# Forgetting attention with a SwiGLU block: tanh's table set loaded later, batch 0's first copies in two parts, first stage in a new order

## The chip, the cores and the metric

The kernel runs on one core of one Trainium2 chip. Its time is device microseconds (us), the median of several runs. The engines are TensorE (PE for matmuls and transposes, PEld for its weight loads), VectorE (DVE), ScalarE (ACT), GpSimd (POOL) and SyncE (SP). All five run at once, each through its own instructions in the order in which they were issued; they wait for one another by semaphores. SP, ACT and POOL also issue the DMAs here.

## The reference

Eight batches with eight heads each, 576 positions, 64 numbers per head; then 4608 tokens of 512 numbers through a SwiGLU block with 1536 hidden columns. Inputs and output are float32.

```
scores = q @ k^T / 8
cum    = cumsum(log(clip(f, 1e-4, 1)))              # one forget gate per position
scores = scores + cum[i] - cum[j], causal, then softmax, then @ v
x      = the heads side by side, [4608, 512]
out    = (silu(x @ w_gate) * (x @ w_val)) @ w_out
```

## The kernel before, in words

**The planner.** The kernel first collects its work as operations and then issues them. `Plan` (L35 to L196) is a list scheduler that runs on the host while the program is built. Each operation has engines on which it may run with a cost for each, operations that it comes after, buffers that it takes and frees, and a key. `plan.run` (L1276) goes through a modelled time: whenever an engine is free by the model, it issues on that engine the ready operation with the lowest key. So costs, keys and ready times set the order of the instructions on every engine and, where an operation has two engines, which of them does it. On the chip each engine then keeps that order and waits where the model was wrong. `ORDER` (L1352) holds a key for each of some 600 operations by its number; where it names an operation, it replaces the key written beside that operation. The memset of `idle` is operation 3: it isn't named in this table and keeps its own key of -1e9 (L526).

**Idle matmuls.** `_fill` (L68) puts matmuls of a constant tile `idle` into gaps that the model sees on PE (`dummy`, L1272), from 0.55 to 22 us of modelled time. They compute nothing that is used. The model doubles PE's costs for the first 6 us (TWARM).

**Logs and gates.** f is loaded in four parts and clipped (L359), ACT takes the logs (L363), DVE sums them up by a scan (L367), splits the sums into bfloat16 parts (`hi` L372 and the following), and ACT or DVE make from them the rows by which a score matmul adds the decays (`choose`, L392 on ACT, L394 on DVE: the picks). This is done in two parts, of 256 and of 320 positions.

**Batch 0.** Its q and k come by POOL's DMAs, two heads groups g of two pairs of heads each. `turn_two` (L558, matmuls at L563) transposes them on PE, for each pair and each of q and k as 18 times two 64 x 64 blocks into one PSUM bank; `straighten_two` (L566) copies the 576 columns of the bank into QK, on ACT (L328) or DVE (L330), whichever the planner finds free. `score2` (L710, matmuls at L722 and L730) makes the scores of two heads at once, in four banks of columns called i = 0 to 3; `soft` (L826) is exp on ACT (`expo`, L738) and the causal mask on POOL (L747); `weigh` (L751, matmul L761) multiplies by v. The scores of i = 0 only need the first 256 positions, yet they wait for all of `q_ready`.

**Batch 1** is transposed on PE as well, with 128 rows at a time (`turn` L574, matmul L579; `straighten` L582). From batch 2 on, transposing DMAs do this (`queries`, L680). v is held in VB, whose padding `blank` fills (L467, L471).

**Feed forward.** `unit` (L1057) is a gate matmul group (L919), tanh on ACT (L930; silu is made of tanh), a value group (L919 too), and two products on DVE (L940, L943). `finish` multiplies by w_out (L985). The first token tile's first four columns groups are done in two halves, 256 wide, later ones are 512 wide. Attention of later batches is mixed in between, so that PE always has either. At the operation ALONE the kernel changes from tanh to Silu (`whole`, L932), with a table load of its own (`turn_table`, L935).

**Table loads.** ACT holds one set of function tables. `o_ln` (L523) is a Ln of one number ahead of all logs, which makes the compiler load the set with Ln; `o_warm` (L531) is an Exp of one number behind the logs, which loads the set with exp and tanh. The exps of i = 0 of batch 0 wait for `o_warm` (in `soft`, L828).

## Time and profile before

| | us |
|---|---|
| median of 3 runs | 376.16 (375.9 to 376.44) |
| profiled execution | 376.5 |
| its span in the trace | 374.5 |
| instructions in the span | 9689 |
| PE busy | 368.0 (98%) |
| DVE busy | 256.9 (69%) |
| ACT busy | 212.5 (57%) |
| POOL busy | 169.5 (45%) |

Times inside the trace count from the span's start. In a timeline row the first two numbers are the start of a run of alike instructions and the time until the last of them ended; then come the engine, the line, the operation, what it writes and reads, the shape and the count, and, in brackets, idle time ahead of it with what ended it. In a row of a view by stages each engine has its busy time and its count of instructions, then the granted clock, a DMA share and GB/s. Matmuls overlap: a group's time divided by its count, less what one takes alone, gives the step from one to the next.

### The profile page before, as it was taken

The page shows a single profiled execution, that of the slowest core. Times are in us where ns is not written, and L with a number is a line of the kernel's source. Part 1 is how long each engine was busy: PE and PEld are TensorE (multiplying, and loading weights), DVE is VectorE, ACT ScalarE, POOL GpSimd, SP SyncE. Part 2 cuts the span into 40 slices and gives each one's busy share as a digit, 9 for nine tenths or more (in the row PEclk, how much of TensorE's full clock was granted, in tenths as well). Part 3 has the DMA queues.
Part 4 walks back from the last instruction along what each step waited for, and adds up shares of the span by engine and source line. Part 5 has one row for each costly group of instructions (what it writes and reads, how often), then busy time and mean ns, then how long its engine had stood idle before and what let it go on. Part 6 is the DMA issues. An engine that isn't in the chain of part 4 may idle for free.

```text
span 374.5 us, 9689 instructions
## 1 busy us (share of the span) xinstructions
PE 368.0 (98%) x3715; PEld 249.2 (67%) x3715; DVE 256.9 (69%) x605; ACT 212.5 (57%) x436; POOL 169.5 (45%) x396
## 2 busy tenths in 40 slices
PE   7899999999999999999999999999999999999996
PEld 5667666455789646875578955587666964584586
DVE  7878987499937699548973769845888246617633
ACT  6999953256755647756566556676874233333321
POOL 8897554135565416684249533566440400040021
PEclk9999999999999999999999999999999999999999
DMA  8999998896959997999979999898530120011012
GB/s 144 190 200 194 206 217 143 169 215 121 174 106 234 212 161 111 170 221 181 200 152 200 126 234 196 155 150 212 105 38 19 58 84 2 1 58 56 0 57 86
DMA packets 125179, 52.04 MB, mean 139 GB/s; under 512 B 111838, under 2 KB 119582, under 8 KB 124366
## 3 DMA queue, kind: packets, MB, share of 16 engines
q1 hardware_dynamic: 108638, 36.15, 50.8%
q0 software_dynamic: 16288, 15.14, 27.1%
q8 instruction: 29, 0.48, 0.6%
q14 instruction: 16, 0.13, 0.1%
q10 hardware_dynamic: 208, 0.14, 0.1%
HBM read 38.56 MB, written 17.07 MB: 149 GB/s over the span
## 4 chain that ended last, share of the span: by engine, by line
PE 93%; ACT 3%; DVE 2%; issue 1%; POOL 0%; DVEq 0%; ACTq 0%
PE ps L919 43%; PE ps L985 17%; PE ps L704 10%; PE ps L761 8%; PE ps L926 6%; PE ps L998 3%; PE ps L992 3%; PE ps L722 1%; PE ps L579 1%; PE ps L778 1%; ACT PT L738 1%; ACT QK L328 1%; PE ps L730 0%; ACT xT L363 0%; ACT PTa L738 0%
## 5 line engine op out<-in xcount | busy, mean ns | idle before, releaser
L738 ACT ACTIVATE PT<-ps 128x384 bf16<-128x384 f32 (+2 forms) x192 | 90.8, 510 | 15.6 <-PE ps L704 10.7
L919 PE MATMUL ps<-xT,wv 128*128 128x512 bf16 (+1 forms) x400 | 99.3, 370 | 0.0
L919 PE MATMUL ps<-xT,wg 128*128 128x512 bf16 (+1 forms) x400 | 99.1, 370 | 0.0
L943 DVE SCALAR_TENSOR_TENSOR hh<-th,ps 128x512 bf16<-128x512 f32 (+1 forms) x100 | 65.9, 662 | 19.4 <-PE ps L919 15.9
L930 ACT ACTIVATE th<-ps 128x512 f32<-128x512 f32 (+1 forms) x82 | 47.2, 577 | 51.5 <-PE ps L919 44.8
L747 POOL TENSOR_SCALAR_AFFINE_SELECT PT<-PT 128x128 bf16<-128x128 bf16 (+1 forms) x192 | 54.6, 291 | 41.6 <-ACT PT L738 35.9
L940 DVE SCALAR_TENSOR_TENSOR th<-th,ps 128x512 f32<-128x512 f32 (+1 forms) x82 | 53.7, 655 | 14.7 <-ACT th L930 14.4
L704 PE MATMUL ps<-QK 68*128 68x256 bf16 x392 | 62.8, 261 | 0.1
L919 PEld LDWEIGHTS <-wg 128*128 128x128 bf16 x400 | 37.7, 97 | 34.2
L919 PEld LDWEIGHTS <-wv 128*128 128x128 bf16 x400 | 37.4, 97 | 34.5
L747 POOL TENSOR_SCALAR_AFFINE_SELECT PTa<-PTa 128x256 bf16<-128x256 bf16 x64 | 26.9, 423 | 63.9 <-ACT PTa L738 62.9
L976 DVE TENSOR_TENSOR su<-hh 128x512 bf16<-128x512 bf16 (+1 forms) x126 | 46.6, 404 | 1.0
L985 PEld LDWEIGHTS <-su 128*128 128x128 bf16 x420 | 40.4, 98 | 5.3
L761 PE MATMUL ps<-VB,PT 128*128 128x65 bf16 x768 | 41.4, 193 | 0.1
L704 PEld LDWEIGHTS <-QK 68*128 68x128 bf16 x392 | 31.8, 97 | 13.9 <-issue 0.3
L1018 POOL TENSOR_TENSOR ot<-ot 128x256 f32<-128x256 f32 x14 | 10.1, 724 | 63.8 <-ACT ot L1011 63.8
L761 PEld LDWEIGHTS <-PT 128*128 128x128 bf16 x768 | 34.1, 97 | 7.0 <-POOL PT L747 1.0
L738 ACT ACTIVATE PTa<-ps 128x384 bf16<-128x384 f32 x64 | 30.9, 488 | 12.6 <-PE ps L704 11.7
L933 ACT ACTIVATE th<-ps 128x512 f32<-128x512 f32 x30 | 17.9, 596 | 33.1 <-PE ps L919 27.7
L773 DVE TENSOR_TENSOR xn<-ps,rc 128x320 bf16<-128x320 f32 (+2 forms) x72 | 32.4, 453 | 2.1
L985 PE MATMUL ps<-wt,su 128*128 128x256 bf16 x252 | 32.9, 272 | 0.0
L1011 ACT ACTIVATE ot<-ps 128x512 f32<-128x512 f32 x28 | 16.7, 597 | 27.9 <-PE ps L985 26.5
(101 smaller groups left out, 407.0 us busy)
## 6 DMA issues: line engine op xcount, KB each, us to landing
out_dram<-ot SPq DMA_DIRECT2D x35, 256.0 KB
natv<-in_v_dram SPq DMA_DIRECT2D x25, 256.0 KB
qk_d<-in_q_dram POOLq DMA_DIRECT2D x24, 144.0 KB, 4.3
qk_d<-in_k_dram POOLq DMA_DIRECT2D x24, 144.0 KB, 4.8
wv<-in_moe_w_val_dram POOLq DMA_DIRECT2D x3, 512.0 KB, 10.7
wg<-in_moe_w_gate_dram POOLq DMA_DIRECT2D x3, 512.0 KB, 12.1
wo<-in_moe_w_out_dram POOLq DMA_DIRECT2D x4, 384.0 KB, 13.7
VB<-in_v_dram POOLq DMA_DIRECT2D x7, 128.0 KB, 9.1
```

What stands on the lines that cost most here:

```text
L704: nc.tensor.matmul(s[:, c : c + w], QK[:KR, hqk[p].i, 1, j * S + kt * P : j * S + (kt + 1) * P], QK[:KR, hqk[p].i, 0, j * S + q0 : j * S + ...
L738: nc.scalar.activation(place(h, i)[:, OFFS[i] : OFFS[i] + c], ps(bs)[:, :c], AF.Exp, scale=0.125)
L747: nc.gpsimd.affine_select(out=d, in_=d, pattern=pat, compare_op=ALU.is_ge, fill=0.0, base=0, channel_multiplier=-1,)
L761: nc.tensor.matmul(o[:, lo : lo + D + 1], pt[:, c : c + P], VB[hvb[b].i][:, kt, hb, : D + 1], start=first and n == 0, stop=last and n == l ...
L773: nc.vector.tensor_mul(XN[bx.i][:, qb : qb + nq, j], o, r)
L919: nc.tensor.matmul(ps(bf)[:, a:b], w[:, ko, fc * P : (fc + 1) * P], xT[:, ko, at : at + b - a], start=ko == 0 and a == 0, stop=ko == KD - ...
L926: nc.tensor.matmul(ps(bf)[:, c * P : (c + 1) * P], w[:, ko, (4 * fq + c) * P : (4 * fq + c + 1) * P], xT[:, ko, lo : lo + P], start=c + ko ...
L930: nc.scalar.activation(TH[bt.i][:, :n], ps(bf)[:, :n], AF.Tanh, scale=0.5)
L940: nc.vector.scalar_tensor_tensor(out=t, in0=t, scalar=1.0, in1=ps(bf)[:, :n], op0=ALU.add, op1=ALU.mult)
L943: nc.vector.scalar_tensor_tensor(out=HH[bh.i][:, r, lo : lo + n], in0=TH[bt.i][:, :n], scalar=by, in1=ps(bf)[:, :n], op0=ALU.mult, op1=ALU ...
L976: E[e].tensor_tensor(out=o, in0=x, in1=y, op=f)
L985: nc.tensor.matmul(ps(bf)[:, c * HALF : (c + 1) * HALF], left(g)[:, q * P : (q + 1) * P], right[:, g], start=opens and g == 0, stop=g == K ...
```

## The change

- `o_ln` and `o_warm` become explicit loads of a table set. The first is a set that holds Ln and Exp both, ahead of the logs. The second, the set with exp and tanh, has another key and a ready time of 24 us in the plan. The exps no longer wait for it; the tanhs of the first token tile do.
- Batch 0's copies of q and k are split in two parts, of 29 of 64 and of 35 of 64 columns blocks (261 and 315 columns of 576). The scores of i = 0 wait for the early parts alone.
- The second heads group of batch 0 (JOINED) is transposed like batch 1, 128 rows at a time: 36 transposes in place of 72, of 5 and of 4 blocks to a bank, 640 and 512 columns, each copied in two parts too.
- The planner adds 0.095 to a PE operation whose kind (paired score, transpose, anything else) differs from the one before (SWITCH), and several modelled costs are changed: clip and ln, the landing of f, a fill of VB, the transposes; the paired score loses 0.105.
- Until 48 us the transposes of batch 0 take a bank of the pool f first, then t (T_BANKS); before it was t first.
- `ORDER` is replaced by a new table, for the new numbers. It names operation 3 too.

The diff, with the two tables of keys cut:

```diff
@@ -174,6 +174,8 @@
                         dur *= self.clock(t)
+                        dur += SWITCH * (o.shape != shape)
+                        shape = o.shape
                         self._fill(idle, busy[e], t)
@@ -185,7 +187,7 @@
                         taken[k] += 1
-                        push(max(end + (0.53 if o.tag == "f" else 0.9), T_SW if e == "POOL" else 0.0), "queue", o)
+                        push(max(end + (0.73 if o.tag == "f" else 0.9), T_SW if e == "POOL" else 0.0), "queue", o)
                         push(busy[e], "wake", None)
@@ -307,6 +309,7 @@
         o.tag, o.packet, o.raw = tag, packet, raw
+        o.shape = tag[0] if "PE" in eng and tag[0] in ("s2", "turn") else None
         return o
@@ -425,9 +428,9 @@
             w = c.stop - c.start
-            a = op(("DVE", 0.03 + w / 960), clip, lf[:D], c, after=lds, key=key - 1 + 0.1 * i, tag="clip")
-            a = op(("ACT", 0.13 + w / 1100), ln, lf[D:], c, lf[:D], after=[a], key=key + 0.1 * i, tag="ln")
-            lns.append(op(("ACT", 0.13 + w / 1100), ln, lf[:D], c, after=[a], key=key + 0.1 * i + 0.01, tag="ln"))
+            a = op(("DVE", 0.12 + w / 960), clip, lf[:D], c, after=lds, key=key - 1 + 0.1 * i, tag="clip")
+            a = op(("ACT", 0.18 + w / 980), ln, lf[D:], c, lf[:D], after=[a], key=key + 0.1 * i, tag="ln")
+            lns.append(op(("ACT", 0.18 + w / 980), ln, lf[:D], c, after=[a], key=key + 0.1 * i + 0.01, tag="ln"))
         for i, c in enumerate(parts):
@@ -520,7 +523,7 @@
     SPLIT = [slice(0, HALF), slice(HALF, S)]
-    o_ln = op(("ACT", 1.5), lambda e: nc.scalar.activation(warm, warm, AF.Ln), key=-30,
+    o_ln = op(("ACT", 1.35), lambda e: nc.scalar.preload_act_table_set("natural_log_exp_and_others"), key=-30,
               after=[op(("DVE", 0.07), lambda e: nc.vector.memset(warm, 1.0), key=-30)])
@@ -528,9 +531,9 @@
     dec0, lns, out0, out1 = gates(SPLIT, -25)
-    o_warm = op(("ACT", 1.4), lambda e: nc.scalar.activation(warm, warm, AF.Exp), after=lns, key=WARM_KEY)
+    o_warm = op(("ACT", 1.35), lambda e: nc.scalar.preload_act_table_set("exp_and_others"), after=lns, key=WARM_KEY, ready=WARM_AT)
     o_rest = op(("DVE", 0.3), blank, "rest", key=QKZ_KEY + 0.1)
-    o_vb = [op({"DVE": 0.4, "ACT": 0.6} if i == 1 else ("DVE", 0.4 if i else 0.12), blank, i, after=[o_ct] if i == 1 else [], key=(-29.5, VB1_KEY)[i] if i < FIRST else 40 + 2000 * i, ready=0 if i == 0 else 4.5 if i < FIRST else 15) for i in range(NVB)]
+    o_vb = [op({"DVE": 0.4, "ACT": 0.72} if i == 1 else ("DVE", 0.4 if i else 0.12), blank, i, after=[o_ct] if i == 1 else [], key=(-29.5, VB1_KEY)[i] if i < FIRST else 40 + 2000 * i, ready=0 if i == 0 else 4.5 if i < FIRST else 15) for i in range(NVB)]
     o_qkz = op(("DVE", 0.3), blank, "qk", key=QKZ_KEY)
@@ -563,11 +568,23 @@
 
-    def straighten_two(e, jj, x, bt):
+    def straighten_two(e, jj, x, c0, c1, bt):
         g, j = divmod(jj, 2)
-        dst = QK[:, hq2[0][g].i, x, j * S : (j + 1) * S].rearrange("p (c t) -> p c t", t=QT)
-        copy(e, dst, ps(bt).bitcast(BF16)[:, :S].rearrange("p (t c) -> p c t", t=QT))
-
+        dst = QK[:, hq2[0][g].i, x, j * S : (j + 1) * S].rearrange("p (c t) -> p c t", t=QT)[:, c0:c1]
+        copy(e, dst, ps(bt).bitcast(BF16)[:, :S].rearrange("p (t c) -> p c t", t=QT)[:, c0:c1])
+
+    def turn_four(e, g, x, n, bt):
+        t0, nt = PH[n]
+        t = ps(bt).bitcast(BF16)
+        for i in range(nt):
+            for u in range(2):
+                nc.tensor.transpose(t[D * u : D * (u + 1), i * P : (i + 1) * P],
+                                    QN[0][2 * g + x][:, u, (t0 + i) * D : (t0 + i + 1) * D], ident)
+
+    def straighten_four(e, g, x, n, c0, c1, bt):
+        t0, nt = PH[n]
+        dst = QK[:, hq2[0][g].i, x, : 2 * S].rearrange("p (j c t) -> p j c t", j=2, t=QT)[:, :, c0:c1, t0 : t0 + nt]
+        copy(e, dst, ps(bt).bitcast(BF16)[:, : nt * P].rearrange("p (t j c) -> p j c t", t=nt, j=2)[:, :, c0:c1])
 
@@ -648,16 +665,22 @@
             o_id.behind.extend(o1)
-        for j in range(2):
-            jj = 2 * g + j
-            q_ready[0, jj] = []
-            for x in range(2):
-                kk = key + STEP[j] + x
-                bt = Buf("t", ("f", TURN_F))
-                o2 = op(("PE", 0.22), turn_two, jj, x, bt, after=[o1[x], o_id], take=[bt], key=kk, tag=("turn", 0, jj, x))
+        for x in range(2):
+            for n in range(2):
+                kk = key + x + 2 * n
+                bt = Buf(*T_BANKS)
+                if g in JOINED:
+                    o2 = op(("PE", 1.48 * mm(*[P] * PH[n][1]) - 0.09), turn_four, g, x, n, bt, after=[o1[x], o_id], take=[bt], key=kk, tag=("turn", 0, g, x, n))
+                else:
+                    o2 = op(("PE", 0.25), turn_two, 2 * g + n, x, bt, after=[o1[x], o_id], take=[bt], key=kk, tag=("turn", 0, g, x, n))
                 turns.append(o2)
-                q_ready[0, jj].append(op({"ACT": act(S), "DVE": dve(S) - 0.02}, straighten_two, jj, x, bt, after=[o2, o_qkz],
-                                         use=[bt, hq2[0][g]], key=kk, tag=("str", 0, jj, x)))
+                for m, (c0, c1) in enumerate(((0, EARLY), (EARLY, QP))):
+                    w = (c1 - c0) * (2 * PH[n][1] if g in JOINED else QT)
+                    fn, args = (straighten_four, (g, x, n, c0, c1, bt)) if g in JOINED else (straighten_two, (2 * g + n, x, c0, c1, bt))
+                    c = op({"ACT": act(w), "DVE": dve(w) - 0.02}, fn, *args, after=[o2, o_qkz],
+                           use=[bt, hq2[0][g]], key=kk + 50 * m, tag=("str", 0, g, x, n, m))
+                    for j in range(2) if g in JOINED else [n]:
+                        q_ready.setdefault((0, 2 * g + j), ([], []))[m].append(c)
 
@@ -666,7 +689,7 @@
                 bt = Buf("t", ("f", TURN_F))
-                o2 = op(("PE", 1.48 * mm(*[P] * nt)), turn, b, g, x, n, bt, after=[o1, o_id], take=[bt], key=S1_KEY + kk, tag=("turn", b, g, x))
+                o2 = op(("PE", 1.48 * mm(*[P] * nt) - 0.09), turn, b, g, x, n, bt, after=[o1, o_id], take=[bt], key=S1_KEY + kk, tag=("turn", b, g, x))
                 turns.append(o2)
@@ -826,7 +849,7 @@
         hp = hpt0[h] if i == 0 else hpt[h]
-        a = x = op(("ACT", act(cols)), expo, h, i, bs, after=[a] + ([x1] if i > 1 else []) + ([o_warm] if h < H and not i else []),
+        a = x = op(("ACT", act(cols)), expo, h, i, bs, after=[a] + ([x1] if i > 1 else []),
                    take=[hp] if i < 2 else [], use=([] if i < 2 else [hp]) + [bs], key=kk, tag=("exp", h, i))
@@ -845,9 +868,9 @@
                     segs = [x[2] for x in BANKS[i]]
-                    cost = mm(*segs) * (3 if jj in (ONEHOT1 if i else ONEHOT) else 2) + 0.105
+                    cost = mm(*segs) * (3 if jj in (ONEHOT1 if i else ONEHOT) else 2)
                     gate_rows = [o_past] + dec0[0][jj] + (dec0[1][jj] if i else [])
-                    a = op(("PE", cost), score2, b, jj, i, bs, after=q_ready[b, jj] + gate_rows, take=bs,
+                    a = op(("PE", cost), score2, b, jj, i, bs, after=q_ready[b, jj][0] + (q_ready[b, jj][1] if i else []) + gate_rows, take=bs,
                            use=[hq2[b][jj // 2]], key=kk + 0.1 * i, tag=("s2", b, jj, i))
@@ -1072,7 +1095,7 @@
         else:
-            b = op(("ACT", act(n)), tanh, n, bg, bt, after=[g], take=[bt], use=[bg], key=-5, tag=("tanh", t, fc))
+            b = op(("ACT", act(n)), tanh, n, bg, bt, after=[g] + ([o_warm] if t == 0 else []), take=[bt], use=[bg], key=-5, tag=("tanh", t, fc))
             before.append(b)
@@ -1329,7 +1352,10 @@
 PART1 = -16
-STEP = (0, 2)
+TURN_F = 48.0
+JOINED = (1,)
+T_BANKS = (("f", TURN_F), "t")
+SWITCH = 0.095
 ONEHOT = (0, 1, 2, 3)
@@ -1337,68 +1363,97 @@
-WARM_KEY = -19.5
+WARM_KEY = -5.5
+WARM_AT = 24.0
...
 ORDER = {
-    0: -100237.9606, 1: -9600.3674, 2: -4.697, 4: -99941.2559, 5: -100237.9606, 6: -99941.2559, 11: -10352.4793, 12: -99941.2569,
...
+    0: 1118.333908, 1: 100917.602429, 2: 131.279958, 3: 100370.002157, 4: 101301.794305, 5: 1653.378181, 6: 100919.942803,
...
 }
```

The order by which the new program issues instructions differs from the old one in the first 100 us or so of PE's work and in one stretch around 137 to 158 us (by the place in PE's order), and is the same elsewhere. DVE's memset of `idle` is at place 20 there, where it was first. Ahead of the first gate matmul stand all scores of batch 0 in both, and the transposes of one head group of batch 1.

6 lines of the change are left out of this document (3 added, 3 removed), and 125 rows, old and new, of the table ORDER.

## The prediction

> **What bounds the kernel now.** I read the page first: its engine lines and its slices.
>
> ```profile
> span 374.5 us, 9689 instructions
> PE 368.0 (98%) x3715; PEld 249.2 (67%) x3715; DVE 256.9 (69%) x605; ACT 212.5 (57%) x436; POOL 169.5 (45%) x396
> ACT  6999953256755647756566556676874233333321
> PEclk9999999999999999999999999999999999999999
> ```
>
> PE is busy for 98% of the span, ACT for 57%; but in slices 2 to 5 (9.4 to 47 us) ACT stands at nine tenths, later it does not. So I asked for the sums of three stages, cut at the first real gate matmul (28.2) and at the first 512 wide one (41.3).
>
> ```profile
> 4.30:28.20 23.90, 21.81 (x450) 15.57 (x449) 19.61 (x71) 22.88 (x52) 21.96 (x47) 1.00 1.43 194
> 28.20:41.30 13.10, 13.10 (x163) 10.51 (x162) 11.21 (x28) 12.64 (x31) 8.71 (x22) 1.00 1.42 198
> 41.30:371.40 330.10, 329.68 (x3094) 220.82 (x3090) 222.93 (x481) 175.47 (x354) 135.70 (x320) 1.00 0.72 134
> ```
>
> The columns are PE, PEld, DVE, ACT and POOL. From 41.3 on PE idles 0.42 of 330 us: nothing that the change does there can save much, and behind batch 1 the two instruction orders are the same but for one stretch. From 4.3 to 28.2 ACT works 22.88 of 23.9: the start is a chain through ACT (logs, copies of q and k, exps), and the moment of the first gate matmul, 28.26, is set by it. Both orders hold the same PE work ahead of that matmul (all scores of batch 0 and the batch 1 transposes of one head group), but for 36 fewer transposes. So the sum is: how much later or earlier the first gate matmul comes, and what is lost between it and 41.3.
>
> The PE timeline of the start, then DVE's and ACT's:
>
> ```profile
> 1.05 4.66 PE L1272 MATMUL ps<-idle 128*128 128x256 bf16 x21 [1.05 <-DVE warm L524]
> 5.72 0.81 PE L563 MATMUL ps<-ident,su 64*64 64x64 bf16 x36
> 6.47 0.72 PE L1272 MATMUL ps<-idle 128*128 128x256 bf16 x5
> 8.16 0.66 PE L563 MATMUL ps<-ident,su 64*64 64x64 bf16 x36 [0.96 <-ACT QK L328]
> 8.75 0.72 PE L1272 MATMUL ps<-idle 128*128 128x256 bf16 x5
> 9.40 0.34 PE L722 MATMUL ps<-QK 64*128 64x256 bf16 x4
> 9.90 0.34 PE L722 MATMUL ps<-QK 64*128 64x256 bf16 x4
> 28.26 0.60 PE L919 MATMUL ps<-xT,wg 128*128 128x256 bf16 x4
> ```
>
> ```profile
> 0.89 0.11 DVE L526 MEMSET idle<- 128x64 f32 x1 [0.89 <-PEq L1425]
> 1.03 0.22 DVE L500 MEMSET hh<- 128x192 f32 x1
> 2.69 0.27 DVE L513 CAST ct<-hh 128x12 f32<-128x12 bf16 x1
> 2.85 0.27 DVE L471 MEMSET QK<- 128x256 uint32 x1
> 3.31 0.28 DVE L467 MEMSET VB<- 64x264 f32 x1
> 8.38 0.86 DVE L367 TENSOR_TENSOR_SCAN xT<-xT 128x320 f32<-128x320 f32 x1
> 9.28 0.81 DVE L372 TENSOR_SCALAR xT<-xT 128x320 bf16<-128x320 f32 x1
> 11.54 0.75 DVE L330 COPY QK<-ps 128x576 bf16<-128x576 bf16 x1
> 13.43 1.03 DVE L394 TENSOR_SCALAR xT<-xT,ct 128x320 bf16<-128x320 f32 x2
> ```
>
> ```profile
> 9.74 0.38 ACT L363 ACTIVATE ot<-ot 128x216 f32<-128x216 f32 x1
> 10.14 1.28 ACT L531 ACT_TABLE_LOAD   x1
> 11.44 0.20 ACT L531 ACTIVATE warm<-warm 1x1 f32<-1x1 f32 x1
> 11.55 0.46 ACT L738 ACTIVATE PTa<-ps 128x384 bf16<-128x384 f32 x1
> 11.92 0.62 ACT L328 ACTIVATE QK<-ps 128x576 bf16<-128x576 bf16 x1
> 12.45 0.46 ACT L738 ACTIVATE PTa<-ps 128x384 bf16<-128x384 f32 x1
> 13.35 0.64 ACT L392 ACTIVATE xT<-xT,ct 128x320 bf16<-128x320 f32 x1
> 13.89 0.83 ACT L738 ACTIVATE PTa<-ps 128x384 bf16<-128x384 f32 x2
> 15.31 1.82 ACT L738 ACTIVATE PTa<-ps 128x384 bf16<-128x384 f32 x4 [0.58 <-PE ps L734]
> 26.54 0.44 ACT L328 ACTIVATE xT<-ps 128x320 bf16<-128x320 bf16 x1
> 27.00 0.74 ACT L328 ACTIVATE QK<-ps 64x512 bf16<-64x512 bf16 x1
> ```
>
> Scores stand ready from 9.9 on, but the first exp runs at 11.55, behind the load of exp's table: that load is on the path today.
>
> **The change part by part.**
>
> *Idle matmuls.* The new keys name the memset of `idle` too: it is no longer DVE's first instruction but stands behind the CAST of `ct`, with the memsets of QK (0.27) and VB (0.28) now ahead. The hh memset at 1.03 so moves by some 0.35 (0.55 less the overlaps), the CAST ends at 3.3 instead of 2.95, and PE, whose first instruction waits for `idle`, starts at 3.4 instead of 1.05. The changed order still has 21 idle matmuls ahead of k's transposes. They took (4.66 - 0.42)/20 = 0.21 each (0.42 is what one takes alone, the rest of 4.66), so k is turned at 3.4 + 4.45 = 7.85, not 5.72, though it has landed. The five at 6.47 step by (0.72 - 0.27)/4 = 0.11: PE's rate doubled about 6.0, 5 us after its first matmul, while PEclk shows 1.00. If that is tied to PE's own work, all 21 run slow (7.85, which I take: it is the same 5 us); if to the launch, 13 do and k is turned at 7.05. Both ends stay for the range.
>
> The Trainium skill, "TensorE: Matmul & The Clock Gate", section "What's actually happening", says that the array runs at half rate until a free-running window of about 3.4 us was busy. The trace agrees: 5 us lie between one window and two. By it the rate doubles here between 6.8 and 10.2, and the first score comes up to 0.7 earlier or 0.8 later than in my sum.
>
> *First score.* Behind k's turn stand 5 idle matmuls, q's turn and 4 more. With the rows: 5.72 to 6.47 is 0.75, 8.75 to 9.40 is 0.65, so q is turned at 7.85 + 0.75 + 0.65 = 9.25, 9.35 with part of it still slow. Its first bank reads back 0.5 later. Each bank is now copied in two parts, and ACT and DVE take turns: DVE's early part waits for ACT's late part of the same bank. ACT's 315 columns cost 0.43 (between 0.44 for 320 and 0.62 for 576), DVE's 261 about 0.43 (0.75 for 576, and ACT's fixed share): the first score runs at 9.35 + 0.5 + 0.45 + 0.5 = 10.8, 1.4 later than now. An exp follows a score by 0.7 (9.40 to 9.90, and 0.2 of drain): 11.5. So the first exp stays where it is, 11.5 against 11.55: the 1.28 + 0.20 that leave this place are spent waiting for PE.
>
> *First exp to first gate matmul*, 11.55 to 28.26 on ACT, which rests in it only once for long (0.58). Added: six joined pieces (1734 columns) for two copies of 576. A copy of 576 steps by 0.53 (11.92 to 12.45), so 0.07 + n/1200; the 64x512 copy, with joined's pattern, takes 0.74 where that line gives 0.60, so 0.07 to 0.15 is fixed: 1.87 to 2.35, I take 2.15, less 1.06 is +1.1. A second 320 wide choice moves from DVE: +0.54 (13.35 to 13.89). ACT's piece of k's second bank waits for DVE's piece of that bank, and DVE has scan, hi, two choices ahead (0.86, 0.81, 1.03, after 11.2): it ends by 13.9 while ACT is ready at 13.4: +0.5 (0 to 0.9). Behind it exps and, in PE's order, the next scores wait. Removed: the stall of 0.58 at 15.31. A 640 wide copy (about 0.65) comes ahead of the gate, a 320 copy (0.44) and one exp (0.4) fall behind it: -0.2. Sum 1.1 + 0.54 + 0.5 - 0.58 - 0.2 = +1.35: the first gate matmul at 29.55.
>
> *Array switches and the new order*:
>
> ```profile
> 24.22 0.54 PE L761 MATMUL ps<-VB,PT 128*128 128x65 bf16 x12
> 24.69 0.34 PE L722 MATMUL ps<-QK 64*128 64x64 bf16 x4
> 29.59 0.53 PE L761 MATMUL ps<-VB,PT 128*128 128x65 bf16 x12
> 29.96 0.60 PE L919 MATMUL ps<-xT,wg 128*128 128x256 bf16 x4
> ```
>
> The same twelve matmuls take 0.47 ahead of a 64 row score, 0.37 ahead of a full one: a switch costs 0.1. The orders have 46 and 36; those ahead of the first gate matmul lie beside ACT's work and save nothing, behind it four transpose groups become two: -0.4. The fewer transposes are ahead too: nothing.
>
> *Table load.* It now stands ahead of the first tanh: 1.28 on ACT. PE has four gate and value groups (1.7 us at 0.11 a matmul) to do meanwhile, the next score waits one exp more: 0, up to 0.4 if they are not all free. Counted at 0.
>
> The Trainium skill, "ScalarE: Activation LUTs", section "What ACT_TABLE_LOAD costs", adds a drain of 1.38 to each load, 2.66 together; the trace does not show it, the load at 10.14 begins 0.02 after the log's end.
>
> *Queues.* POOL issues the weights for the second gate columns earlier, the second batch 1 group later; with DMA at 194 to 198 GB/s until 41 the order of landing changes and not the sum, and what is used first lands first. 0, up to 0.4.
>
> Sum: -0.05 + 1.35 - 0.4 = **+0.9**. The profiled execution took 376.5, 2.0 around its span; the median 376.16 is 0.34 below it. 377.4 for such an execution, 377.1 for the median.
>
> **Rivals.** (a) *Absorbed*: the half rate ends early (k at 7.05, first score 0.7 earlier): 377.1 - 0.7 = 376.4. For it: nothing shows what the rate is tied to. (b) *Faster*: the load leaves the path and DVE is not in the way. It decides at the first exp: if that starts before 10.9, at 10.5, say, by early rate and by DVE's early copies not waiting (-1.0), and DVE's piece is done in time (-0.5; the 0.81 of hi may be 0.33, as other 320 wide ones), and the order mixes better behind the gate (-0.4), it is 375.2. Against: DVE's copy waits for ACT's in the order. (c) *Load dearer*: the load drains a full ACT, or exp from the shared set takes longer than 0.46 for 384 columns: at 1.4 more, 378.5. (d) The change doesn't do what it says: both orders hold three loads, so it moves one and drops none; that is in the sum already.
>
> **How the numbers follow.** Forecast 0.52, around +0.9, a quarter of it under +0.75; (a) 0.17; (b) 0.23, a tenth of it under 0.75 of gain; (c) 0.08. About 0.2%, 0.75 us, is what a measurement of this kernel can tell from no change. Slower 0.39 + 0.08 = 0.47; same 0.13 + 0.17 + 0.02 = 0.32; faster 0.21. The range: down to (b) with the joined copies at their low end (0.3), 374.9; up by the late rate (+0.8) and by DVE's wait and the queues (+0.7 together) to 378.6.
>
> **What would show it.** First idle matmul at 3.4; k's turn at 7.85; first score 10.8, first exp 11.5, first gate matmul 29.55; one table load near 29.6 with PE busy over it. An exp before 10.9 makes (b) right; idle matmuls at 0.11 from the ninth or so make (a); an unbroken ACT from 11.5 on refutes the wait for DVE.

## The result, and the profile after

The changed kernel takes 377.5 us (median of 20 runs, 376.13 to 379.19), the kernel before 376.18 (20 runs, 375.89 to 377.79): a ratio of 1.0033, 95% interval 1.002 to 1.0047, so 1.3 us slower. A second series gave 377.24 against 376.23, ratio 1.0031 (1.0016 to 1.0046). The profiled execution took 378.53, 1 us above its median, with a span of 376.5.

The page of the changed kernel, the lines that answer to those of before:

```profile
span 376.5 us, 9579 instructions
PE 365.0 (97%) x3643; PEld 248.7 (66%) x3677; DVE 256.9 (68%) x607; ACT 212.8 (57%) x440; POOL 169.1 (45%) x396
ACT  4999875255755647755576556577774233323321
PEclk9999999999999999999999999999999999999999
```

PE has 2 idle matmuls and 36 transposes fewer (PEld 3677 for 3715; 34 more records of PE are missing, so its busy time can't be compared). ACT is busy for as long as before.

PE's timeline of the start, DVE's rows around the memset of `idle`, and ACT's, in the changed kernel:

```profile
3.74 4.66 PE L1295 MATMUL ps<-idle 128*128 128x256 bf16 x21 [3.74 <-DVE VB L470]
8.33 0.66 PE L568 MATMUL ps<-ident,su 64*64 64x64 bf16 x36
8.92 0.72 PE L1295 MATMUL ps<-idle 128*128 128x256 bf16 x5
9.57 0.66 PE L568 MATMUL ps<-ident,su 64*64 64x64 bf16 x36
11.03 0.34 PE L745 MATMUL ps<-QK 64*128 64x256 bf16 x4 [0.26 <-DVE QK L333]
29.40 0.60 PE L942 MATMUL ps<-xT,wg 128*128 128x256 bf16 x4
```

```profile
3.56 0.11 DVE L529 MEMSET idle<- 128x64 f32 x1
10.54 0.77 DVE L333 COPY QK<-ps 128x261 bf16<-128x261 bf16 x2 [2.13 <-ACT QK L331]
```

```profile
11.72 0.87 ACT L761 ACTIVATE PTa<-ps 128x384 bf16<-128x384 f32 x2 [0.29 <-PE ps L757]
12.48 0.66 ACT L395 ACTIVATE xT<-xT,ct 128x320 bf16<-128x320 f32 x1
13.76 0.71 ACT L331 ACTIVATE QK<-ps 128x232 bf16<-128x232 bf16 x2 [0.25 <-DVE QK L333]
14.31 0.49 ACT L761 ACTIVATE PTa<-ps 128x384 bf16<-128x384 f32 x1
14.67 1.56 ACT L331 ACTIVATE QK<-ps 128x350 bf16<-128x350 bf16 x4
16.00 0.70 ACT L395 ACTIVATE xT<-xT,ct 128x320 bf16<-128x320 f32 x1
28.82 1.28 ACT L534 ACT_TABLE_LOAD   x1
```

The path can be read across the three: the memset of `idle` at 3.56 starts PE at 3.74, PE's idle matmuls hold k's transposes until 8.33, DVE's copy of the early part waits 2.13 for ACT's copy of the late part of the same bank, the first score comes at 11.03, and ACT stands idle for 0.29 ahead of the first exp, at 11.72 where it was at 11.55. No load stands there any more. The first gate matmul comes at 29.40, 1.14 later than in the kernel before. The load of exp's and tanh's set lies at 28.82, and PE has gate and value groups over it.

Later the two kernels do the same work. ACT's tanh rows around 74 us, of the changed kernel and of the kernel before:

```profile
74.60 0.60 ACT L953 ACTIVATE th<-ps 128x512 f32<-128x512 f32 x1 [0.27 <-PE ps L942]
```

```profile
74.12 0.60 ACT L930 ACTIVATE th<-ps 128x512 f32<-128x512 f32 x1 [0.27 <-PE ps L919]
```

Only 0.48 of the 1.14 is left there: by then the order behind the first gate matmul has given 0.66 back. Some 0.2 is lost again between 100 and 165 us, so that at the last copies of the output the changed kernel is 0.66 later. Its span is 2.0 longer, though. The rest, 1.3, is spent behind all engine work. SP's waits at the end, of the changed kernel and of the kernel before:

```profile
SPq L1491 <- DMA out_dram<-ot: 2.1, 3, 1.7
```

```profile
SPq L1436 <- DMA out_dram<-ot: 0.8, 3, 0.4
```

The three last stores are waited for 2.1 in place of 0.8, one of them 1.7. The view of the DMA queues of the changed kernel between 373.30 and 373.40 shows what runs beside it:

```profile
q8 instruction: 1, 0.02, 70.0%
```

This is a fetch of instructions for PE: one packet of 16 KB, 1.12 us long, on one of the 16 DMA engines. The last store was issued at 372.60. Eight of its packets run from 374.46 on, as the fetch ends (374.47), where all others had ended by 373.79; its last landing comes at 375.50, the ones before that by 374.15. In the kernel before the last such packet starts at 367.77, ahead of the last store. These packets come about every 256 PE instructions (each matmul and each weight load is one). PE's program is now 76 instructions shorter, so that the same fetch, counted back from the end, comes 33 instructions ahead of it by that count, where it was 109. In the trace it starts 1.1 behind PE's last matmul, which ends at 372.25.

### The profile page after: what moved, and what is told of

The parts are those of the page before. It is cut to its first block, busy times and chain, and to the rows that moved or that the text cites. A ratio compares the mean times of both kernels' runs of the same rounds, so it can differ in the third digit from the quotient of the medians.

```text
span 376.5 us, 9579 instructions
## 1 busy us (share of the span) xinstructions
PE 365.0 (97%) x3643; PEld 248.7 (66%) x3677; DVE 256.9 (68%) x607; ACT 212.8 (57%) x440; POOL 169.1 (45%) x396
## 4 chain that ended last, share of the span: by engine, by line
PE 92%; DVE 4%; ACT 2%; issue 1%; POOL 0%; DVEq 0%
PE ps L942 43%; PE ps L1008 17%; PE ps L727 10%; PE ps L784 8%; PE ps L949 6%; PE ps L1021 3%; PE ps L1015 3%; PE ps L1295 1%; DVE QK L333 1%; PE ps L801 1%; ACT QK L331 1%; PE ps L745 1%; PE ps L596 0%; DVE xn L796 0%; PE ps L753 0%
## 5 line engine op out<-in xcount | busy, mean ns | idle before, releaser
L761 ACT ACTIVATE PT<-ps 128x512 bf16<-128x512 f32 (+2 forms) x192 | 90.4, 513 | 16.5 <-PE ps L727 13.1
L942 PE MATMUL ps<-xT,wv 128*128 128x512 bf16 (+1 forms) x385 | 97.0, 370 | 0.9
L942 PE MATMUL ps<-xT,wg 128*128 128x512 bf16 (+1 forms) x384 | 96.7, 370 | 0.9
L770 POOL TENSOR_SCALAR_AFFINE_SELECT PT<-PT 128x128 bf16<-128x128 bf16 (+1 forms) x192 | 53.0, 282 | 43.3 <-ACT PT L761 37.2
L784 PE MATMUL ps<-VB,PT 128*128 128x65 bf16 x768 | 42.3, 193 | 0.2
```

The lines of the kernel that those rows point to most:

```text
L761: nc.scalar.activation(place(h, i)[:, OFFS[i] : OFFS[i] + c], ps(bs)[:, :c], AF.Exp, scale=0.125)
L770: nc.gpsimd.affine_select(out=d, in_=d, pattern=pat, compare_op=ALU.is_ge, fill=0.0, base=0, channel_multiplier=-1,)
L784: nc.tensor.matmul(o[:, lo : lo + D + 1], pt[:, c : c + P], VB[hvb[b].i][:, kt, hb, : D + 1], start=first and n == 0, stop=last and n == l ...
L942: nc.tensor.matmul(ps(bf)[:, a:b], w[:, ko, fc * P : (fc + 1) * P], xT[:, ko, at : at + b - a], start=ko == 0 and a == 0, stop=ko == KD - ...
```

## The experiments

Theory A: the prediction's steps make about +0.65 in the first stage (late idle matmuls, more copies on ACT, against a load that leaves the path), and what goes beyond is the last instruction fetch beside the last store. Theory B, its rival: the fetch is a chance of one execution, and all of the difference comes from the first stage. Theories C (a fetch also makes PE wait in the first stage) and D (PE's rate falls when it rests) arose on the way. All changes were made so that each engine's other instructions kept their order.

**1. The changed kernel with 84 more PE instructions.**

```diff
-        nc.tensor.matmul(z[:, :HALF], idle, idle.unsqueeze(1).to_broadcast([P, 2, P]), start=True, stop=True)
+        calls.append(i)
+        if len(calls) > 30:
+            for c in range(4):
+                nc.tensor.matmul(z[:, 64 * c : 64 * (c + 1)], idle, idle[:, :64], start=True, stop=True)
+        else:
+            nc.tensor.matmul(z[:, :HALF], idle, idle.unsqueeze(1).to_broadcast([P, 2, P]), start=True, stop=True)
```

> The changed kernel with its last 14 idle matmuls (256 columns) cut into four of 64 columns each: the same columns at the same places, but 84 more PE instructions ahead of everything from the first FFN groups on. Theory A (the change costs about 0.65 us in the first stage; what the median shows beyond that, and the spread of 376.1 to 379.2, is PE's last 16 KB instruction fetch, which runs beside the last store because the changed program has 76 PE instructions fewer): the last fetch falls some 4 to 6 us ahead of the end of the span, the wait for the last store is back to about 1.2 us, the median is 376.6 to 376.9 and the runs lie within 0.8 of each other. Theory B (fetch and store are a chance of the one profiled execution; the median and the spread come from the first stage): 377.3 to 377.7, with a spread of 2 to 3 us as before.

Measured: 377.33 (376.48 to 378.86, 12 runs) against 376.46, ratio 1.0020 (1.0007 to 1.0033). In its profile PE follows that of the changed kernel to within 0.05 all the way, the last fetch starts at 368.15, and the span is 375.1 in place of 376.5. SP's waits at its end:

```profile
SPq L1498 <- DMA out_dram<-ot: 0.8, 3, 0.4
```

So the same work ends 1.4 earlier when the fetch doesn't meet the store: for the profiled execution Theory A holds. For the median it isn't settled. The ratio fell from 1.0033 to 1.0020, but the intervals overlap, the median of 377.33 lies 0.4 above what A gave, and the runs spread by 2.4, not 0.8.

**2. The kernel before with 180 more PE instructions**, to bring the fetch to its end.

```diff
-        nc.tensor.matmul(z[:, :HALF], idle, idle.unsqueeze(1).to_broadcast([P, 2, P]), start=True, stop=True)
+        calls.append(i)
+        if len(calls) > 31:
+            for c in range(7):
+                nc.tensor.matmul(z[:, 16 * c : 16 * (c + 1)], idle, idle[:, :16], start=True, stop=True)
+        else:
+            nc.tensor.matmul(z[:, :HALF], idle, idle.unsqueeze(1).to_broadcast([P, 2, P]), start=True, stop=True)
```

> The kernel before with its last 15 idle matmuls (256 columns) replaced by seven of 16 columns each: 180 more PE instructions, so that, counted back from the program's end, a 16 KB fetch boundary lies where the changed kernel has it (33 instructions ahead of the end; 109 in the kernel before). The first stage stays as it is up to 0.2 us. Theory A: the last fetch runs within the last 4 us and meets the last store, so the median rises by 0.3 to 1.3, to 376.5 to 377.5, and the spread grows from 0.6 to 2 us or more. Theory B: 376.0 to 376.4, spread as before.

Measured: 380.3 (379.89 to 380.7, 5 runs), ratio 1.0097 (1.0078 to 1.0117), outside what either theory gave. The last fetch ran at 379.13, behind the span's end at 378.0, and met nothing. The time was lost in the first stage: the first gate matmul comes at 31.73, 3.47 later than in the kernel before. The larger part of it is a rest of PE. Its timeline there:

```profile
11.16 0.86 PE L1277 MATMUL ps<-idle 128*128 128x16 bf16 x28
11.95 0.41 PE L563 MATMUL ps<-ident,su 64*64 64x64 bf16 x14
14.76 0.32 PE L563 MATMUL ps<-ident,su 64*64 64x64 bf16 x4 [2.40 <-issue]
```

PE rests for 2.40 in the middle of 18 transposes, and nothing that the profile shows holds it ("issue"). The matmul at 14.76 is the 223rd counted from 0. The kernel before has such a rest too, in a row that the prediction didn't look for:

```profile
15.01 0.21 PE L733 MATMUL ps<-one,xT 64*128 64x128 bf16 x1 [0.68 <-issue]
```

That is its matmul 223 as well, with other work (a score, not a transpose). So it isn't the work that waits, it is the place in the program. The first 16 KB fetch runs from 12.51 to 13.44 here, from 12.74 to 13.63 in the kernel before, and PE goes on 1.32 and 1.38 behind its end. That is Theory C.

The smaller part is PE's rate. From 13.25 to 20.07, around and behind the rest, the granted clock is 0.50, so the next scores run at half their rate. The mean granted clock of all five runs is 0.991 to 0.995, where 24 of the 29 runs of the kernel before have 0.998 or more.

**3. The changed kernel with the memset of `idle` first.**

```diff
-    op(("DVE", 0.12), lambda e: nc.vector.memset(idle.bitcast(F32), ONE2), key=-1e9, tag="idle")
+    nc.vector.memset(idle.bitcast(F32), ONE2)
+    op(("DVE", 0.12), lambda e: None, key=-1e9, tag="idle")
...
```

(with the edit of the first experiment)

> The changed kernel, with the 84 more PE instructions, and with the memset of idle as DVE's first instruction again; every other instruction keeps its place. Theory A with the prediction's first step (the first score waits for the idle matmuls, which start 2.4 us late because of that memset): idle matmuls from about 1.1, k turned at about 5.9, the first score at about 9.3, the first exp at about 10 in place of 11.72, the first gate matmul 0.8 to 1.6 earlier than 29.4; median 375.0 to 376.0. Rival (ACT or DVE have a chain of their own of the same length, logs and gate rows, or the rate doubles by the clock of the launch): the first gate matmul moves by under 0.4, the median is that of the same kernel with the memset late, 376.6 to 376.9.

Measured: 375.76 (375.3 to 377.55, 12 runs) against 376.46, ratio 0.998 (0.9966 to 0.9993): 1.6 below the same kernel with the memset late, and faster than the kernel before. One memset of 0.11 us, 2.5 us too late on an engine that isn't the bottleneck, was worth more than the whole loss. Its PE timeline:

```profile
1.06 4.33 PE L1303 MATMUL ps<-idle 128*128 128x256 bf16 x21 [1.06 <-DVE idle L529]
6.45 0.66 PE L569 MATMUL ps<-ident,su 64*64 64x64 bf16 x36 [1.07 <-DMA su<-in_k_dram]
7.04 0.72 PE L1303 MATMUL ps<-idle 128*128 128x256 bf16 x5
8.85 1.04 PE L1303 MATMUL ps<-idle 128*128 128x256 bf16 x4
9.82 0.50 PE L746 MATMUL ps<-QK 64*128 64x256 bf16 x4
28.79 0.60 PE L943 MATMUL ps<-xT,wg 128*128 128x256 bf16 x4
```

k's transposes now wait for k itself, which lands at 6.4. The first gate matmul came 0.61 earlier, less than hoped, and the rows say why: the five idle matmuls at 7.04 step by 0.11, the four at 8.85 by some 0.2. PE had rested 1.07 ahead of 6.45, and later ran at half its rate again; the first exp came at 11.0, not at 10. The granted clock is 0.50 from 8.32 to 11.73, and the row of clocks by slices of 9.4 us dips in the second:

```profile
PEclk9899999999999999999999999999999999999999
```

That is Theory D. It isn't how most executions of this kernel run, though: of the twelve only the profiled one (376.5) and that of 377.55 have a mean granted clock of 0.994 and 0.995, the ten others have 0.999 or 1.0 and lie at 375.3 to 376.19. And a rest alone doesn't do it: PE rests for 0.96 in the kernel before (ahead of 8.16) and for 1.46 in the fourth experiment (ahead of 6.46), and in their profiles the clock doesn't fall.

**4. The kernel before with the table loads alone changed.**

```diff
-    o_ln = op(("ACT", 1.5), lambda e: nc.scalar.activation(warm, warm, AF.Ln), key=-30,
+    o_ln = op(("ACT", 1.5), lambda e: nc.scalar.preload_act_table_set("natural_log_exp_and_others"), key=-30,
...
-    o_warm = op(("ACT", 1.4), lambda e: nc.scalar.activation(warm, warm, AF.Exp), after=lns, key=WARM_KEY)
+    o_warm = op(("ACT", 1.4), lambda e: None, after=lns, key=WARM_KEY)
...
     def tanh(e, n, bf, bt):
+        if not loaded:
+            loaded.append(nc.scalar.preload_act_table_set("exp_and_others"))
```

> The kernel before with the table loads alone changed, every other instruction at its place: the set with log and exp first, the set with exp and tanh straight ahead of the first tanh. Theory A (the load ahead of the first exp is on the path in the kernel before: scores are ready at 9.9, the first exp runs at 11.55): the first exp at 10.2 to 10.5, the first gate matmul 0.8 to 1.4 earlier than 28.26, the load near 27.5 covered by PE up to 0.5; median 375.0 to 375.6. Rival 1 (the load costs on ACT near 28 what it saved, since ACT is busy for 12.6 of 13.1 us there): 376.0 to 376.4. Rival 2 (exp from the shared set takes longer): the exps of 384 columns over 0.5 instead of 0.46.

Measured: 377.3 (377.13 to 378.15, 12 runs) against 376.46, ratio 1.0024 (1.0011 to 1.0037): slower, which none of the three had. Its ACT and its PE:

```profile
10.36 0.49 ACT L738 ACTIVATE PTa<-ps 128x384 bf16<-128x384 f32 x1 [0.47 <-PE ps L734]
15.61 1.82 ACT L738 ACTIVATE PTa<-ps 128x384 bf16<-128x384 f32 x4 [1.09 <-PE ps L734]
29.47 1.28 ACT L933 ACT_TABLE_LOAD   x1
```

```profile
15.30 0.21 PE L733 MATMUL ps<-one,xT 64*128 64x128 bf16 x1 [0.98 <-issue]
28.56 0.60 PE L919 MATMUL ps<-xT,wg 128*128 128x256 bf16 x4
31.95 0.60 PE L919 MATMUL ps<-xT,wg 128*128 128x256 bf16 x4 [0.69 <-ACT QK L328]
```

The first exp did come 1.2 earlier, at 10.36. But PE rests at matmul 223 until 15.30 (the first fetch ended at 13.95), and ACT waits for it at 15.61: the gain ends there. And in this order the load at 29.47 isn't free: ACT's copies of batch 1 stand behind it, PE waits for them for 0.69, and by 35 us PE is 1.79 later than before. Rival 2 isn't seen: the eight exps of 384 columns into PTa ahead of the first gate matmul take 0.487 each, 0.476 in the kernel before; that also speaks against the second half of the prediction's rival (c). So the load's move is worth something only where no fetch holds PE, and is hidden only where PE has work that needs nothing of ACT. The changed kernel's order gives both.

**5. The changed kernel once more**, for a second profile.

> The changed kernel, unchanged, for a second profile and its spread. What is fixed by the program: the last 16 KB fetch for PE begins behind PE's last matmul. Theory A (fetch and last store meet by the program's length, and by how much differs from run to run): PE's last matmul about 0.65 later than in the kernel before, the fetch again between 1 us ahead of and 2 us behind the last store's issue, the wait for that store between 1.2 and 3.5; runs spread over 2 to 3 us, the median 0.3 to 0.6 above that of the same kernel with 84 more PE instructions (377.33). Theory B (a chance): wait of about 1.2 and a median within 0.2 of 377.33.

Measured: 377.24 (376.44 to 379.25, 12 runs) against 376.23. The median is 0.09 from 377.33, as Theory B had it; Theory A had put it 0.3 to 0.6 above. The profiled execution is the fastest, 376.44:

```profile
3.73 3.78 PE L1295 MATMUL ps<-idle 128*128 128x256 bf16 x21 [3.73 <-DVE VB L470]
7.44 0.66 PE L568 MATMUL ps<-ident,su 64*64 64x64 bf16 x36
10.14 0.34 PE L745 MATMUL ps<-QK 64*128 64x256 bf16 x4 [0.26 <-DVE QK L333]
```

PE starts at the same moment as in the first profile and does the same 21 idle matmuls in 3.78 in place of 4.66: its rate doubled earlier. The trace's entries for the granted clock begin at that moment, at 6.46 here and at 8.34 in the first profile. The views count the time ahead of the first entry as full speed, so a row of nines can stand over a start at half rate. The first score comes 0.89 earlier, and PE stays 0.87 to 0.99 ahead of the first profile to the end. In five profiles in which the memset is late and the 21 matmuls start at 3.73 or 3.74, they took 4.66, 3.78, 4.62, 3.86 and 4.57 (the first profile, this one, and experiments 1, 7 and 8). The expectation that PE's last matmul is fixed at +0.65 was wrong. The last fetch here starts at 375.37, behind the last store, and SP's waits are 0.8 in all: no meeting. So both ends of the kernel differ from run to run: in the changed kernel k's transposes stand behind PE's slow phase, in the kernel before they wait for k, and the slow phase doesn't show.

**6. The kernel before with 23 idle matmuls of 512 columns** in place of 46 of 256.

```diff
-        nc.tensor.matmul(z[:, :HALF], idle, idle.unsqueeze(1).to_broadcast([P, 2, P]), start=True, stop=True)
+        calls.append(i)
+        if len(calls) % 2:
+            nc.tensor.matmul(z[:, :MT], idle, idle.unsqueeze(1).to_broadcast([P, 4, P]), start=True, stop=True)
```

> The kernel before with each two idle matmuls of 256 columns made one of 512: 23 in place of 46, the same columns, 46 PE instructions fewer, nothing else changed. Theory C (the wait of 0.68 in PE ahead of its matmul number 223 is the first 16 KB instruction fetch: in three runs with different work at that number it ended 1.35 to 1.38 behind the fetch's end): the wait moves 23 matmuls further on, to work that PE reaches later, and is under 0.2; ACT's idle 0.58 at 15.3 goes; the first gate matmul 0.3 to 0.6 earlier than 28.26, the median 0.2 to 0.6 lower than before. Rival (PE waits there for a bank or a semaphore that the profile doesn't show): the wait stays ahead of the same score, 0.5 to 1.0, and the median within 0.2 of before.

Measured: 375.73 (375.2 to 376.84, 11 runs) against 376.23, ratio 0.9986 (0.9972 to 0.9999). Its PE and ACT:

```profile
14.34 0.34 PE L761 MATMUL ps<-VB,PTa 128*128 128x65 bf16 x6 [0.43 <-DMA VB<-in_v_dram]
27.54 0.60 PE L919 MATMUL ps<-xT,wg 128*128 128x256 bf16 x4
```

```profile
11.14 0.46 ACT L738 ACTIVATE PTa<-ps 128x384 bf16<-128x384 f32 x1
13.48 1.57 ACT L738 ACTIVATE PTa<-ps 128x384 bf16<-128x384 f32 x4
```

No "issue" wait is left, ACT's exps run on from 13.48, and the first gate matmul is 0.72 earlier: 0.41 of it at the first exp, where this execution was ahead already, and 0.31 behind it. PE now waits 0.43 for v. Its matmul 223 runs at 15.20, 2.0 behind the end of its first packet (13.19). Theory C holds: the rest of 0.68 was the first instruction fetch.

**7. The changed kernel with the load ahead of the first exp.**

```diff
-    o_warm = op(("ACT", 1.35), lambda e: nc.scalar.preload_act_table_set("exp_and_others"), after=lns, key=WARM_KEY, ready=WARM_AT)
+    o_warm = op(("ACT", 1.35), lambda e: None, after=lns, key=WARM_KEY, ready=WARM_AT)
...
     def expo(e, h, i, bs):
+        if not loaded:
+            loaded.append(nc.scalar.preload_act_table_set("exp_and_others"))
```

(with the edit of the first experiment)

> The changed kernel (with the 84 more PE instructions) with the set of exp and tanh loaded ahead of the first exp, as in the kernel before, and not ahead of the first tanh; all else at its place. By the prediction (a load is on the path ahead of the first exp, and hidden ahead of the first tanh, since PE has four groups to do): the first exp at 12.7 in place of 11.72, the first gate matmul 0.6 to 1.1 later than 29.4, no gain from the load that is gone there; median 0.6 to 1.1 above the same kernel with the load late (377.33). Rival (the load costs the same at both places, or DVE's copy and PE are late anyway): within 0.3 of it.

Measured: 378.37 (377.69 to 378.77, 5 runs) against 376.23, ratio 1.0058 (1.0045 to 1.0071), against 1.0020 with the load late: 0.38%, 1.4 us by the ratios, 1.04 by the two medians as they stand (the kernel before stood at 376.23 in one series and at 376.46 in the other). In its ACT timeline the load lies at 10.76 and the first exp at 12.06; its first gate matmul comes at 29.87. The profile of the fifth experiment, with its early double rate, is the one to compare with: there the first exp is at 10.83, the first gate matmul at 28.54, 1.23 and 1.33 earlier. The two profiles stay 1.3 to 1.5 apart from there to the end. So within the changed kernel the moved load is worth 1.0 to 1.4, about all that was hoped of it, and costs nothing that can be seen where it went.

**8. The changed kernel with whole copies for the first head group.**

```diff
     def straighten_two(e, jj, x, c0, c1, bt):
+        if c0:
+            return
+        c1 = QP
```

(with the edit of the first experiment)

> The changed kernel (with the 84 more PE instructions) with the first head group's four banks copied whole, 576 columns, at the place and on the engine of the early part, and no late parts. By the prediction (the early part on DVE only runs once ACT has done the late part of the same bank, so the split gains nothing): the first score within 0.3 of 11.03, DVE's copies without the wait of 2.13 for ACT but 0.2 longer each, median within 0.4 of the same kernel with two parts (377.33). Rival (two parts bring the first score forward): the first score 0.4 to 0.8 later, median 0.4 to 0.9 higher.

Measured: 377.19 (376.65 to 377.71, 6 runs) against 376.23, ratio 1.0027 (1.0016 to 1.0038), where two parts gave 1.0020. In its profile, a late doubling like the first one's, the first score runs at 10.80 in place of 11.03, the first gate matmul at 29.52 in place of 29.40. DVE's copies start when q is turned:

```profile
9.99 1.42 DVE L333 COPY QK<-ps 128x576 bf16<-128x576 bf16 x2 [1.74 <-PE ps L568]
```

The split into two parts gains nothing that can be measured.

**9. Idle matmuls over the gap ahead of k.** The third experiment's kernel with `for _ in range(9 if len(calls) == 21 else 1)` ahead of its matmul of 256 columns: eight more behind the first 21.

> The changed kernel with the memset of idle first (and the 84 more PE instructions), and eight more idle matmuls of 256 columns behind the first 21, so that PE doesn't stand idle from 5.4 to 6.45, when k lands. Theory D (PE's rate fell back to half from about 8.4 to 11.6 in the same kernel without them, because PE had rested for 1.07 us: its scores step by 0.21 there and not 0.11): all matmuls from k's turn on at the full rate, the first score at 9.2 to 9.5 in place of 9.82, the first exp at 9.9 to 10.3 in place of 11.0, the first gate matmul 0.3 to 0.8 earlier; median 375.0 to 375.5, 0.3 to 0.7 below the same kernel without them (375.76). Rival (the half rate there has another cause, or DVE and ACT are late at 13 to 15 anyway): slow scores again, or a median within 0.2 of 375.76; if k lands early, the eight cost up to 0.4.

Measured: 376.31 (375.9 to 376.52, 11 runs) against 376.42, ratio 0.9990 (0.9976 to 1.0004). The clock did what D says: PE ran through to 6.95, all later groups step at the full rate, the first score came at 9.65, the first exp at 10.34 (11.0 without the eight), and no run has a granted clock under 0.999. But the median isn't lower: it is 0.55 above the third experiment's 375.76. Ten of that kernel's twelve runs had no fall of the clock that the eight could mend. PE at the second head group:

```profile
14.38 0.27 PE L746 MATMUL ps<-QK 64*128 64x256 bf16 x1 [0.57 <-DVE QK L333]
15.01 0.27 PE L746 MATMUL ps<-QK 64*128 64x256 bf16 x2 [0.37 <-issue]
28.60 0.60 PE L943 MATMUL ps<-xT,wg 128*128 128x256 bf16 x4
```

Matmul 223 again, until 15.01, 1.6 behind the end of the first fetch (13.40). The first gate matmul gained only 0.19 on that of the third experiment's profile. That the wait at 223 makes up the 0.55 isn't shown: there is no profile of the third experiment's kernel without the fall.

**10. The kernel before with the memset of `idle` late.**

```diff
-    op(("DVE", 0.12), lambda e: nc.vector.memset(idle.bitcast(F32), ONE2), key=-1e9, tag="idle")
+    op(("DVE", 0.12), lambda e: None, key=-1e9, tag="idle")
...
             nc.vector.tensor_copy(one, zt.rearrange("p (k c) -> p k c", c=32)[:, 4:8, 0])
+            nc.vector.memset(idle.bitcast(F32), ONE2)
```

> The kernel before with the memset of idle moved behind the copies of ct and one, as the changed kernel has it; nothing else changed. By the prediction's first step (the idle matmuls start late, and k is turned late): idle matmuls from 3.2, k turned at 7.1 to 7.9 in place of 5.7 to 6.4, ACT's four copies, log and load behind it all later, the first exp 0.4 to 1.2 later than 11.55; median 0.3 to 1.0 above before. Rival (the load ahead of the first exp, or the wait for the instruction fetch, hides it): within 0.2.

Measured: 377.08 (376.43 to 377.77, 12 runs) against 376.42, ratio 1.0014 (1.0 to 1.0028), +0.5 to 0.7. In the profile the idle matmuls start at 3.26 and take 4.08, k is turned at 7.27, the first exp runs at 11.90, the first gate matmul at 28.51, 0.25 later than before, in an execution whose rate doubled early. As in the prediction's first step, and smaller than in the changed kernel; the rest at matmul 223 follows here too (0.58, until 15.26).

**11. The memset first, and 512 columns to an idle matmul.** The memset's edit of the third experiment, the edit of the sixth, and `for _ in range(4 if len(calls) == 21 else 1)` ahead of its matmul.

> The changed kernel with the memset of idle first, and its idle matmuls as 512 columns in place of each two of 256, three more behind the first 11: the same idle columns as in the run with eight more, 39 and 95 PE instructions fewer than in the changed kernel and in that run. Theory C with D (in that run PE waited again at matmul 223, to 15.01, 1.6 us behind the end of the first 16 KB instruction fetch; and the full rate is kept): no wait at matmul 223, the second head group's scores at about 14.4, exps from 15.0 in place of 15.61, the first gate matmul 0.3 to 0.6 earlier than in that run, median 0.7 to 1.1 below the kernel before (0.11 below it in that run). Rival (the wait at 223 hides one of DVE that stays): within 0.2 of that run, 0 to 0.3 below before. The last fetch for PE may again meet the last store, or fall behind the end.

Measured: 376.36 (375.46 to 378.5, 12 runs) against 376.41, ratio 1.0005 (0.9989 to 1.0021). The first stage came out as C and D together say: no "issue" wait, exps of the second head group from 15.00, and

```profile
27.86 0.60 PE L943 MATMUL ps<-xT,wg 128*128 128x256 bf16 x4
```

0.74 ahead of the ninth experiment, 1.54 ahead of the changed kernel. The lead holds until 98 us and is lost there in one place. DVE's and POOL's timelines:

```profile
98.58 2.30 DVE L1000 TENSOR_TENSOR su<-hh 128x512 bf16<-128x512 bf16 x1
```

```profile
98.13 1.18 POOL L333 CAST VB<-natv 128x512 bf16<-128x512 f32 x2
99.25 0.29 POOL L771 TENSOR_SCALAR_AFFINE_SELECT PT<-PT 128x128 bf16<-128x128 bf16 x1
99.51 0.40 POOL L771 TENSOR_SCALAR_AFFINE_SELECT PTa<-PTa 128x256 bf16<-128x256 bf16 x1
99.87 0.73 POOL L771 TENSOR_SCALAR_AFFINE_SELECT PT<-PT 128x128 bf16<-128x128 bf16 x3
```

This sum of 512 columns, 0.42 in the middle of its 84 in this kernel, takes 2.30 while POOL casts v and masks, and ends 0.28 behind POOL's last mask; PE waits for DVE three times in the next 5 us and comes out 0.27 behind the ninth experiment. The meeting itself isn't new: in each of the twelve other profiles the sum that starts under these two casts takes 1.02 to 1.29. Here it is 1.28 longer than in the ninth. Half of the runs (375.46 to 375.95) look like ones in which it is short, but only one was profiled, so that is left open.

## Why the prediction came out as it did

The forecast was +0.9 (377.1, slower); measured is +1.3 (377.5), inside the range. The chain was right; the sum holds a term too large, a term read wrongly, and lacks one. That the number comes so near is partly luck. Up to the last copy the first profile has +0.66 (+0.17 to the first exp, +0.97 to the gate, -0.48 behind it) where the sum had +0.9 (-0.05, +1.35, -0.4), and what lies behind that copy wasn't forecast.

- **Idle matmuls, right.** 3.4 and 7.85 were forecast, 3.74 and 8.33 measured, as the memset came at 3.56. "All 21 run slow", which I took, held in the first profile and in those of experiments 1 and 8. In the fifth experiment they took 3.78: the rival *absorbed* gave 376.4 for an early doubling, and that execution took 376.44. Both happen, from run to run. The sign that was named for the rival *faster*, a first exp ahead of 10.9, stands in that execution too (10.83), at 376.44 and not at 375.2: it only tells an early doubling from a late one. The rate is tied to neither PE's first matmul nor the launch. The Trainium skill, "TensorE: Matmul & The Clock Gate", section "What's actually happening", calls the activity window free-running. The five times above, for one and the same start, agree: the granted clock begins at 8.34, 6.46, 8.18, 6.61 and 8.07.
- **First score and exp, right.** 10.8 and 11.5 against 11.03 and 11.72, DVE waiting for ACT's late part as said. Experiments 3 and 8 show that the idle matmuls set it and the split doesn't matter.
- **From exp to gate, mis-sized.** +1.35 was forecast, +0.97 measured (17.68 less 16.71). The six joined pieces take 1.88 (13.76 to 14.31 and 14.67 to 16.00), which is the low bound and not the 2.15 that I took; the wait for DVE was 0.25, not 0.5. Removing "the stall of 0.58" was right, but I had not asked what it was. It was PE's first instruction fetch (experiments 2 and 6). In the changed kernel 38 matmuls are fewer ahead of the same work, and matmul 223 comes at 18.33, 3.57 behind the end of the first packet (14.76): nothing waits. "The start is a chain through ACT" was thus only half the truth, and experiment 4, argued by that chain, went the other way.
- **Switches and the new order, about right.** -0.4 was forecast; -0.66 came by 74 us, and -0.48 is left of it at the last copy. No run took the switches and the new order apart.
- **The load, right.** Free at its new place in the new order, 1.0 to 1.4 at the old one (experiment 7); in the order of the kernel before it isn't free there (experiment 4). That the memset takes the gain away was the point of the forecast, and experiments 3 and 10 show it from both sides.
- **What lay behind the last copy, missing.** The sum ended with PE. A last instruction fetch beside the last store added 1.3 to the profiled execution. Of the three profiles with 33 instructions by the count it met the store in that one alone; in the two others (experiments 2 and 5) it started behind the span's end. How much of the median it makes isn't settled: experiment 5 came out as Theory B had it; of 32 runs of the changed kernel seven lie above 378.5, 1.1 above the median; of the five kernels with 84 more instructions two of 46 lie 1.2 above their own. It may explain the top of the spread, and at best a few tenths of the median.

By these terms, +0.66 at the last copy, and 0.3 because the profiled execution of before lay above its median, executions like the first profile should lie at 377.15 without that fetch, and those with an early doubling lie lower; what the median of 377.5 has above that, 0.35 or more, stays unattributed.

The best version is the third experiment's, 0.7 below the kernel before (ratio 0.998); the sixth's, 0.5 below (0.9986), can't be told from it by the intervals.

## What to carry over

When an order is made anew, look first at the smallest instructions that other engines' first work waits for: one 0.11 us memset decided the sign here. A wait whose releaser the profile gives as "issue" deserves a question before it enters a sum: compare the instruction's number in the program between versions. And end the sum at the last store's landing, not at the last matmul; the number of instructions is part of a change.

## What the runs showed of the hardware

- PE reads its program by packets of 16 KB, about one for every 256 instructions, and rests when one is late: at its matmul 223 in five kernels, with three kinds of work there, until 1.3 to 1.6 us behind the end of the first packet, for 0.37 to 2.40. The Trainium skill, "Runtime: NRT & Kernel Launch", section "Instruction fetch mechanics", says that crossing such a boundary is mostly hidden. The trace differs for the first boundary; the later ones are hidden here.
- Such a packet takes about 1 us of one DMA engine; one landing of a 64 KB store beside it came 1.35 behind the others.
- PE's rate doubled 2.7 to 4.6 us after its first matmul, for the same start. It fell back to half for 3.41 us behind a rest of 1.07 in experiment 3 (by the granted clock of the runs in two of twelve), and for 6.82 us around a rest of 2.40 in experiment 2 (by it in all five), but not behind rests of 0.96 and 1.46 in two other profiles: what decides stays open.
- A DVE sum of two tiles, 0.42 for 512 columns, took 2.30 beside casts and masks on POOL in one profile, and 1.02 to 1.29 beside the same casts in the twelve others. The Trainium skill, "SBUF — State Buffer", section "SBUF: two separate sides", tells of a pair of ports that a DVE instruction with two inputs in SBUF shares with a GpSimd instruction that reads SBUF, and that the first of them holds for the whole instruction. That would fit; no run here took the POOL work away, so the cause isn't shown.
